# Joining the two words of a float64 weight with one two-input integer operation, the sign moved by a parametric ReLU

## The chip, the cores and the metric

One core of a Trainium2 chip runs the whole program. The metric is device time in microseconds (us), median over runs. Five engines work side by side, each in its own program order: TensorE (PE, with its weight loads as PEld), VectorE (DVE), ScalarE (ACT), GpSimd (POOL) and SyncE (SP, here only a DMA queue).

## The reference, cut to what matters

The inputs are float32 activations and float64 weights. Attention with queries averaged in pairs is followed by two feed-forward blocks on 1152 tokens of 512 numbers:

```
attn = softmax(scale * mean2(q) @ k.T) @ v          # 2 x 8 heads
xn   = x / sqrt(mean(x*x) + 1e-6) * rms_g
x    = (silu(xn @ w_gate) * (xn @ w_val)) @ w_out   # 512 -> 1536 -> 512
h    = x @ w_in
out  = (h * tanh(softplus(h))) @ w_out2             # 512 -> 2048 -> 512
```

## The kernel before, in words

Every product is made of three half-precision matmuls: each factor is split into a high part and the low rest. So each weight block needs a float32 number first, and this kernel makes it from the two 32-bit words of the float64.

**A job** (`w1_job`, `wo_job`, `w2i_job`, `w2o_job`; 68 in all) treats 512 numbers for each of 128 partitions. `w_load` brings both words by DMA into a `raw` tile (four buffers), word 0 the low and word 1 the high one. `w_a` (L395) reads the high word as a float32 and multiplies it by 2^-111 on ACT into `gx` (two buffers); that takes 111 from its exponent field. `w_b` (L401) makes the float32 pattern on DVE into `c` (two buffers) with three operations: L408 shifts `gx` left by 3 and clears the top bit, L411 puts the sign bit of `gx` in, L414 puts the upper three bits of the low word in. `w_c` (L418) rounds `c` to the high part on ACT (L421) and takes the low part by a subtraction on POOL (`lo_op`, L134).

**The order** is written out by hand; every engine takes its instructions in the order of the program. There are four stretches:

- Attention, to about 257 us: 72 steps (`attn_step`). DVE takes row maxima (L267) out of PSUM, ACT the exponentials (L274) and the split of them (L287, L314). Four jobs run here, in pieces (`job_piece`, L449): one call of `w_b` in a step, so the three operations of L408, L411 and L414 fall in three steps, and the fourth step has `w_c` of this job and `w_a` of the next. Each piece stands at the end of its step.
- The first block's two input products, from 258 to 411 us: a unit (`unit1`) is 24 matmuls of 288 columns into two of six PSUM buffers (`pg`, `pv`). ACT applies silu (L572), DVE multiplies (`fo`, L574) and so sets the two buffers free, ACT and POOL split the product (L581, L134). After each unit `job_step` (L434) issues `w_c` of the job two back, `w_b` of the one before, `w_a` of the current one and the load of a later one. So `fo` of a unit stands on DVE behind the operations of the job of the step before.
- The first block's output product, to 484 us: `unit1o` is 36 matmuls of 288 columns into one of the six buffers, set free by `y` on DVE (L136, called from L613). In the first six units two jobs are treated each.
- The second block, from 484 us: 48 steps of 12 matmuls of 384 columns (`h_mm`), mish on ACT (L648), a split on ACT and DVE, and 9 matmuls of 512 columns (`o_part`), with a job in each of the first steps while there are any.

Activation tables are loaded at L758, twice at L572, at L840 and at L894.

Of the kernel before, what the change touches and what calls it, by code (L numbers as in the profile page):

```python
# [9 lines left out]
F32 = mybir.dt.float32  # L10
F16 = mybir.dt.float16
I32 = mybir.dt.int32
ACTF = mybir.ActivationFunctionType
ALU = mybir.AluOpType
# [26 lines left out]
def kernel(  # L41
# [13 lines left out]
    nc = tc.nc  # L55
# [339 lines left out]
    def w_a(job):  # L395
        t = job["raw"]
        gx = raw_p.tile([128, t.shape[1], t.shape[2]], F32, tag="gx", name="gx")
        nc.scalar.activation(out=gx, in_=t[:, :, :, 1].bitcast(F32), func=ACTF.Copy, scale=2.0 ** -111)
        job["g"] = gx

    def w_b(job, part=None):  # L401

        t, g = job["raw"], job["g"].bitcast(I32)
        if part in (None, 0):
            job["c"] = raw_p.tile([128, t.shape[1], t.shape[2]], I32, tag="c", name="c")
        c = job["c"]
        if part in (None, 0):
            nc.vector.tensor_scalar(out=c, in0=g, scalar1=3, scalar2=0x7FFFFFFF,  # L408
                                    op0=ALU.logical_shift_left, op1=ALU.bitwise_and)
        if part in (None, 1):  # L410
            nc.vector.scalar_tensor_tensor(out=c, in0=g, scalar=-0x80000000, in1=c,  # L411
                                           op0=ALU.bitwise_and, op1=ALU.bitwise_or)
        if part in (None, 2):
            nc.vector.scalar_tensor_tensor(out=c, in0=t[:, :, :, 0], scalar=29, in1=c,  # L414
                                           op0=ALU.logical_shift_right, op1=ALU.bitwise_or)
            del job["raw"], job["g"]

    def w_c(job):  # L418
        hi, lo = job["to"]()
        cf = job.pop("c").bitcast(F32)  # L420
        nc.scalar.activation(out=hi, in_=cf, func=ACTF.Copy)  # L421
        lo_op(job.get("eng", nc.gpsimd), lo, cf, 1.0, hi)

    jobs = []
    jn = [0, 0, 0, 0]

    def job_load(upto):
        while jn[0] < min(upto, len(jobs)):
            jobs[jn[0]]["raw"] = jobs[jn[0]]["load"]()
            jn[0] += 1  # L430
# [3 lines left out]
    def job_step(k=1):  # L434

        for _ in range(k):
            if jn[3] < jn[2]:
                w_c(jobs[jn[3]])
                jn[3] += 1
            if jn[2] < jn[1]:  # L440
                w_b(jobs[jn[2]])
                jn[2] += 1
            if jn[1] < len(jobs):
                job_load(jn[1] + 1)
                w_a(jobs[jn[1]])
                jn[1] += 1
            job_load(jn[1] + AHEAD)

    def job_piece(k):  # L449

        i, p = divmod(k, 4)
        if p == 0 and i:
            w_c(jobs[i - 1])
            jn[3] += 1
        if i == NE:
            return
        if p == 0:
            w_a(jobs[i])
            jn[1] += 1
            job_load(jn[1] + AHEAD)  # L460
        elif p == 1:
            w_b(jobs[i], 0)
        else:
            w_b(jobs[i], p - 1)
            jn[2] += p == 3


    ss_t, rw = {}, {}
# [288 lines left out]
    with tc.manual_schedule():  # L757
# [25 lines left out]
        for n in range(NIT):  # L783
            attn_step(n)
            if rs:
                rs.pop(0)()
            if n == RMS0:
                rs = rms_steps(0, 0, NI + 1, 2)
            if n == JOBL:
                job_load(AHEAD)  # L790
            if 0 <= n - JOB0 <= 4 * NE:
                job_piece(n - JOB0)
# [98 lines left out]
        m_p = pool("m", 3)  # L891
        ot_p = pool("ot", 2)

        nc.scalar.preload_act_table_set("mish")  # L894
        hs = [(c, f) for c in range(NC) for f in range(F2)]
        PARTS = 8
        NO = CH // 128
# [50 lines left out]
```

## Time and profile before

| | |
|---|---|
| three runs | 674.79, 675.17, 677.33 us; median 675.17 |
| profiled execution, first to last instruction | 674.8 us |
| mean granted TensorE clock | 0.987 |
| busy: PE, PEld | 605.0 us (90%), 421.6 us (62%) |
| busy: DVE, ACT, POOL | 449.9 (67%), 392.4 (58%), 328.3 us (49%) |
| chain that ended last, by engine | PE 49%, DVE 28%, ACT 8%, issue 8%, DMA 4%, POOL 2% |

The page gives no time around the span, so the span stands for the profiled execution; it is within 0.4 us of the median. A matmul's record is longer than the distance to the next one, since matmuls are pipelined, so how full PE is has to be read from starts and counts. An operation's record includes the time for which it is held up after it was issued.

### The profile page before, as it was taken

Reading aid. Unit: us, or ns where it says so; the run is one execution under the profiler, and the core shown is the slowest. Engines: PE = TensorE matmul, PEld = TensorE weight load, DVE = VectorE, ACT = ScalarE, POOL = GpSimd, SP = SyncE. Lnnn points to the kernel's source line nnn. Section 1 sums busy time; section 2 is a strip of 40 time slices with the busy share of each in tenths; the row PEclk is TensorE's granted clock in tenths of the full one; section 3 lists DMA queues with packets and bytes.
Section 4 is the critical chain, followed back from the end, with each engine's and each line's share of the span. In section 5 each row is a group of like instructions: output and inputs, shape, how many; then the busy total and the mean of one; then the engine's idle time right before and its main releaser. Section 6 shows DMA issues by size and latency. Waiting matters only on the chain.

```text
span 674.8 us, 14672 instructions
## 1 busy us (share of the span) xinstructions
PE 605.0 (90%) x5880; PEld 421.6 (62%) x5880; DVE 449.9 (67%) x740; ACT 392.4 (58%) x659; POOL 328.3 (49%) x260
## 2 busy tenths in 40 slices
PE   3688888888867788899999999999999999999997
PEld 2466566666645567677777677777755555555553
DVE  3889998989969996769999922488299911111110
ACT  4888898998968887655555541344356623223221
POOL 0778878688889752467878741344133300000000
PEclk9899999999988899999999999999999999999999
DMA  6799999999998997625555512156055101001001
GB/s 190 123 211 189 186 183 185 197 182 186 204 203 163 174 161 147 132 94 157 159 157 169 158 47 63 39 182 187 17 169 159 64 0 48 1 1 32 16 1 47
DMA packets 161908, 84.05 MB, mean 125 GB/s; under 512 B 124720, under 2 KB 152368, under 8 KB 161840
## 3 DMA queue, kind: packets, MB, share of 16 engines
q1 hardware_dynamic: 151184, 67.71, 47.0%
q10 hardware_dynamic: 10656, 15.40, 8.4%
q8 instruction: 46, 0.75, 0.5%
q14 instruction: 22, 0.18, 0.1%
HBM read 50.07 MB, written 2.36 MB: 78 GB/s over the span
## 4 chain that ended last, share of the span: by engine, by line
PE 49%; DVE 28%; ACT 8%; issue 8%; DMA 4%; POOL 2%; ACTq 1%; SPq 0%; DVEq 0%; POOLq 0%
DVE m L267 8%; DVE c L411 6%; PE z L544 5%; PE z L546 5%; PE z L545 5%; PE po L681 4%; PE po L680 4%; PE po L679 4%; ACT e L274 3%; PE py L544 3%; PE py L546 3%; PE py L545 3%; DVE c L408 3%; DMA et<-hl 3%; DVE et L134 2%
## 5 line engine op out<-in xcount | busy, mean ns | idle before, releaser
L134 POOL TENSOR_TENSOR hl<-e,hl 128x768 f16<-128x768 f32 x71 | 117.5, 1655 | 60.5 <-ACT hl L287 37.0
L267 DVE TENSOR_REDUCE m<-s 128x1 f32<-128x1152 f32 x72 | 97.3, 1351 | 8.9 <-PE s L249 7.6
L274 ACT ACTIVATE e<-s,m 128x1152 f32<-128x1152 f32 x72 | 87.7, 1218 | 18.8 <-DVE m L268 17.6
L249 PE MATMUL s<-kqT 128*128 128x384 f16 (+1 forms) x480 | 87.9, 336 | 9.6 <-DVE kqT L203 7.5
L136 DVE SCALAR_TENSOR_TENSOR g<-mo,g 128x384 f16<-128x384 f32 x48 | 26.9, 562 | 100.5 <-ACT g L654 100.5
L411 DVE SCALAR_TENSOR_TENSOR c<-gx,c 128x512 int32<-128x512 int32 x68 | 75.7, 1114 | 2.2
L338 PE MATMUL av<-vv,et 128*128 128x65 f16 (+1 forms) x720 | 75.4, 195 | 1.8 <-DMA et<-hl 1.0
L134 POOL TENSOR_TENSOR stretch<-c,stretch 128x512 f16<-128x512 f32 x40 | 51.3, 1283 | 52.0 <-ACT stretch L421 51.8
L414 DVE SCALAR_TENSOR_TENSOR c<-raw,c 128x512 int32<-128x512 int32 x68 | 75.0, 1103 | 2.2
L340 PE MATMUL av<-vv,et 128*128 128x64 f16 (+1 forms) x720 | 75.3, 194 | 0.0
L341 PE MATMUL av<-vv,et 128*128 128x65 f16 (+1 forms) x720 | 75.1, 196 | 0.0
L338 PEld LDWEIGHTS <-et 128*128 128x128 f16 (+1 forms) x720 | 68.0, 102 | 3.6 <-issue 2.3
L340 PEld LDWEIGHTS <-et 128*128 128x128 f16 (+1 forms) x720 | 67.8, 101 | 0.8
L341 PEld LDWEIGHTS <-et 128*128 128x128 f16 (+1 forms) x720 | 67.8, 101 | 0.0
L134 POOL TENSOR_TENSOR h<-fo,h 128x288 f16<-128x288 f32 x48 | 48.8, 1016 | 36.3 <-ACT h L581 36.3
L648 ACT ACTIVATE mo<-z 128x384 f32<-128x384 f32 x48 | 23.3, 484 | 71.3 <-PE z L546 71.3
L287 ACT ACTIVATE hl<-e 128x768 f16<-128x768 f32 x72 | 60.7, 843 | 3.5 <-DMA et<-hl 1.4
L544 PE MATMUL z<-y,w2i 128*128 128x384 f16 x192 | 62.6, 326 | 0.0
L545 PE MATMUL z<-y,w2i 128*128 128x384 f16 x192 | 62.6, 326 | 0.0
L546 PE MATMUL z<-y,w2i 128*128 128x384 f16 x192 | 62.6, 326 | 0.0
L309 PE MATMUL ep<-idf,e 128*128 128x128 f32 x216 | 39.0, 291 | 24.7 <-ACT e L274 23.5
L249 PEld LDWEIGHTS <-kqT 128*128 128x128 f16 (+1 forms) x480 | 40.2, 102 | 33.1 <-issue 15.6
(106 smaller groups left out, 1570.0 us busy)
## 6 DMA issues: line engine op xcount, KB each, us to landing
raw<-in_moe_w_out_dram SPq DMA_DIRECT2D x28, 512.0 KB, 3.4
raw<-in_moe_w_in_dram SPq DMA_DIRECT2D x16, 512.0 KB, 3.7
raw<-in_moe_w_gate_dram SPq DMA_DIRECT2D x8, 512.0 KB, 3.6
raw<-in_moe_w_val_dram SPq DMA_DIRECT2D x8, 512.0 KB, 3.5
vn<-in_v_dram ACTq DMA_DIRECT2D x14, 288.0 KB, 2.9
kn<-in_k_dram ACTq DMA_DIRECT2D x12, 288.0 KB, 4.5
qn<-in_q_dram ACTq DMA_DIRECT2D x12, 256.0 KB, 3.4
raw<-in_moe_w_gate_dram ACTq DMA_DIRECT2D x4, 512.0 KB, 5.0
```

What stands on the lines that cost most here:

```text
L134: eng.tensor_tensor(out=out_, in0=in_, in1=hi, op=ALU.subtract)
L249: mm = nc.tensor.matmul(out=ps[p0:p0 + m, c, 0:SN], lhsT=qt[:, w * NTI + slot, p0:p0 + m], rhs=kt[:, e * NJ + c * per:e * NJ + (c + 1) * p ...
L267: nc.vector.tensor_reduce(out=m[:, 0:1], in_=ps[:, :, 0:SN], op=ALU.max, axis=AXL.XY, negate=True)
L274: nc.scalar.activation(out=e.rearrange("p (c s) -> p c s", c=SC), in_=ps[:, :, 0:SN], func=ACTF.Exp, bias=m[:, 1:2], scale=s_scale)
L338: nc.tensor.matmul(out=av[0:m, o0:o0 + D + 1], lhsT=hi, rhs=vr[:, D:2 * D + 1], start=(jj == 0), stop=False)
L340: nc.tensor.matmul(out=av[0:m, o0:o0 + D], lhsT=hi, rhs=vr[:, 0:D], start=False, stop=False)
L341: nc.tensor.matmul(out=av[0:m, o0:o0 + D + 1], lhsT=et[:, z + (NB if jj < NB else PB), p0:p0 + m], rhs=vr[:, D:2 * D + 1], start=False, st ...
L411: nc.vector.scalar_tensor_tensor(out=c, in0=g, scalar=-0x80000000, in1=c, op0=ALU.bitwise_and, op1=ALU.bitwise_or)
L414: nc.vector.scalar_tensor_tensor(out=c, in0=t[:, :, :, 0], scalar=29, in1=c, op0=ALU.logical_shift_right, op1=ALU.bitwise_or)
L544: nc.tensor.matmul(out=ps, lhsT=w0, rhs=x0, start=(i == 0), stop=False)
L545: nc.tensor.matmul(out=ps, lhsT=w0, rhs=x1, start=False, stop=False)
L546: nc.tensor.matmul(out=ps, lhsT=w1, rhs=x0, start=False, stop=(i == n - 1))
```

## The change

`w_a` uses a parametric ReLU with the factor -(2^32) on negative numbers in place of a copy. A negative number comes out positive with 32 added to its exponent field, so that bit 28 of `gx` carries the sign, and a shift left by 3 brings it to bit 31. `w_b` has two operations: the low word is shifted right by 29 into `c`, and `gx` shifted left by 3 is joined with it. The low word's shift reads every second word of `raw`. In the pieces of the attention stage the two operations take the places of the first and the second, and the third place is empty. The activation table loaded ahead of the second block is named `mish_and_others`, not `mish`.

```
-        nc.scalar.activation(out=gx, in_=t[:, :, :, 1].bitcast(F32), func=ACTF.Copy, scale=2.0 ** -111)
+        nc.scalar.activation(out=gx, in_=t[:, :, :, 1].bitcast(F32), func=ACTF.Prelu, scale=2.0 ** -111,
+                             alpha=-(2.0 ** 32))
...
         if part in (None, 0):
-            nc.vector.tensor_scalar(out=c, in0=g, scalar1=3, scalar2=0x7FFFFFFF,
-                                    op0=ALU.logical_shift_left, op1=ALU.bitwise_and)
+            nc.vector.tensor_scalar(out=c, in0=t[:, :, :, 0], scalar1=29, scalar2=None,
+                                    op0=ALU.logical_shift_right)
         if part in (None, 1):
-            nc.vector.scalar_tensor_tensor(out=c, in0=g, scalar=-0x80000000, in1=c,
-                                           op0=ALU.bitwise_and, op1=ALU.bitwise_or)
-        if part in (None, 2):
-            nc.vector.scalar_tensor_tensor(out=c, in0=t[:, :, :, 0], scalar=29, in1=c,
-                                           op0=ALU.logical_shift_right, op1=ALU.bitwise_or)
+            nc.vector.scalar_tensor_tensor(out=c, in0=g, scalar=3, in1=c,
+                                           op0=ALU.logical_shift_left, op1=ALU.bitwise_or)
             del job["raw"], job["g"]
...
-        elif p == 1:
-            w_b(jobs[i], 0)
-        else:
+        elif p < 3:
             w_b(jobs[i], p - 1)
-            jn[2] += p == 3
+            jn[2] += p == 2
...
-        nc.scalar.preload_act_table_set("mish")
+        nc.scalar.preload_act_table_set("mish_and_others")
```

## Rows read from the trace of the kernel before

**Rows 1.** Busy time by stretch: us, then PE, PEld, DVE, ACT, POOL busy, PEclk, DMA.
```profile
320.00:340.00 20.00, 20.00 (x165) 15.96 (x164) 19.59 (x26) 11.17 (x25) 15.29 (x12) 1.00 0.51 159
360.00:380.00 20.00, 18.66 (x148) 14.13 (x146) 19.55 (x26) 11.22 (x26) 15.39 (x13) 1.00 0.52 159
520.00:540.00 20.00, 20.00 (x110) 10.55 (x108) 18.60 (x24) 11.97 (x25) 7.77 (x7) 1.00 0.26 80
```

**Rows 2.** Waits of PE, 255 to 675 us: total us, times, longest.
```profile
PE pv L544 <- DVE fo L574: 2.3, 5, 0.5
PE py L544 <- DVE y L136: 1.9, 2, 1.0
PE pv L546 <- POOL stretch L134: 1.2, 1, 1.2
```

**Rows 3.** Timeline of PE around two of its waits: start, us, instruction, [idle before].
```profile
283.96 0.29 PE L545 MATMUL pv<-stretch 128*128 128x288 f16 x1
285.48 0.30 PE L546 MATMUL pv<-stretch 128*128 128x288 f16 x1 [1.24 <-POOL stretch L134]
...
358.98 0.29 PE L546 MATMUL pg<-stretch 128*128 128x288 f16 x1
359.73 0.28 PE L544 MATMUL pv<-stretch 128*128 128x288 f16 x1 [0.46 <-DVE fo L574]
```

**Rows 4.** Groups by line and shape, whole span: busy us, mean ns, idle before.
```profile
L411 DVE SCALAR_TENSOR_TENSOR c<-gx,c 128x512 int32<-128x512 int32 x68 | 75.7, 1114 | 2.2
L414 DVE SCALAR_TENSOR_TENSOR c<-raw,c 128x512 int32<-128x512 int32 x68 | 75.0, 1103 | 2.2
...
L398 ACT ACTIVATE gx<-raw 128x512 f32<-128x512 f32 x68 | 45.1, 666 | 0.0
...
L408 DVE TENSOR_SCALAR c<-gx 128x512 int32<-128x512 int32 x68 | 37.7, 554 | 19.5 <-POOL woh L134 15.6 <-ACT gx L398 2.9 <-POOL w2i L134 1.0
...
L141 DVE TENSOR_SCALAR vn<-vn 128x1152 f32<-128x1152 f32 x7 | 5.3, 753 | 0.0
...
L516 ACT ACTIVATE xh<-xn,w 128x512 f16<-128x512 f32 x4 | 2.8, 714 | 2.4 <-DVE xn L507 2.4
...
L572 ACT ACT_TABLE_LOAD x2 | 2.6, 1283 | 0.0
...
L516 ACT ACTIVATE xh<-xn 128x512 f16<-128x512 f32 x4 | 2.5, 631 | 0.1
```

**Rows 5.** Timeline of DVE, two units of the first block.
```profile
302.76 0.44 DVE L574 SCALAR_TENSOR_TENSOR fo<-ft,pv 128x288 f32<-128x288 f32 x1
...
303.74 1.54 DVE L411 SCALAR_TENSOR_TENSOR c<-gx,c 128x512 int32<-128x512 int32 x1
305.32 1.10 DVE L414 SCALAR_TENSOR_TENSOR c<-raw,c 128x512 int32<-128x512 int32 x1
306.34 0.44 DVE L574 SCALAR_TENSOR_TENSOR fo<-ft,pv 128x288 f32<-128x288 f32 x1
...
307.15 0.69 DVE L411 SCALAR_TENSOR_TENSOR c<-gx,c 128x512 int32<-128x512 int32 x1
...
309.34 0.44 DVE L574 SCALAR_TENSOR_TENSOR fo<-ft,pv 128x288 f32<-128x288 f32 x1
```

**Rows 6.** Timeline of POOL, beside those units, and one product's low part alone.
```profile
289.54 0.73 POOL L134 TENSOR_TENSOR h<-fo,h 128x288 f16<-128x288 f32 x1 [0.59 <-ACT h L581]
...
303.58 1.16 POOL L134 TENSOR_TENSOR stretch<-c,stretch 128x512 f16<-128x512 f32 x1
```

**Rows 7.** Timeline of ACT in attention: exponentials behind the steps with L414.
```profile
227.73 1.22 ACT L274 ACTIVATE e<-s,m 128x1152 f32<-128x1152 f32 x1 [0.20 <-DVE m L268]
...
240.35 1.22 ACT L274 ACTIVATE e<-s,m 128x1152 f32<-128x1152 f32 x1 [0.37 <-DVE m L268]
...
252.96 1.22 ACT L274 ACTIVATE e<-s,m 128x1152 f32<-128x1152 f32 x1 [0.34 <-DVE m L268]
```

**Rows 8.** Timeline of DVE at the first block's start.
```profile
281.88 1.10 DVE L414 SCALAR_TENSOR_TENSOR c<-raw,c 128x512 int32<-128x512 int32 x1
```

## The prediction

> **What bounds the kernel now.** I read the busy time by stretch first, then the waits of PE, then the timelines of the engines that it waits for. The reader is to see that the kernel has three regimes, and that only two of them can give anything back.
>
> From 484 us on, PE is never idle although DVE is 93% busy (the third row) [rows 1]. Nothing that DVE does less of there is worth anything. In the first block's input products PE is at its limit too at first: 165 matmuls in 20 us are 0.121 us each, so a unit of 24 takes 2.91 us at full granted clock [rows 1]. But DVE needs longer: two units start 6.58 us apart, 3.29 us each, without a gap [rows 5]. PE runs ahead of DVE by its six PSUM buffers until they are used up; then it issues fewer matmuls in a stretch (the second row) [rows 1] and waits for `fo` five times. So DVE is the bound there, with PE close behind. The list of waits names all that PE loses to DVE's work on weights: `fo` five times, `y` twice, and once a low part of a weight that POOL makes late because DVE was late [rows 2]. In attention PE waits for ACT and DVE in turn; there the reader looks at ACT's exponentials and at what was still missing when they started [rows 7].
>
> **What it removes.** One of three DVE operations of a job goes, 68 in all. By its record each of the two-input ones is 1.10 to 1.11 us on average [rows 4], so DVE loses some 75 us of busy time. Very little of that is on the path. Stage by stage:
>
> *Attention, four jobs.* The step with L414 loses it. The next exponential on ACT had waited for DVE for 0.20, 0.37 and 0.34 us in three of these steps [rows 7]; in the fourth ACT had no such wait. Behind these waits ACT is the next late one (exponential, split and transposed part follow each other without a gap), so what goes is the wait and not the whole operation: 0.9 us. Bounds: 0 if the PE or a transposing DMA is late instead, and 4 x 1.10 = 4.4 us if DVE is the only bound. I take 0.9, since the rows show the wait itself.
>
> *Start of the first block.* PE stands from one matmul to the next for 1.52 us where 0.12 is normal, a loss of 1.40 us, for the low part of a weight [rows 3]. Ahead of that part stand L414 with 1.10 us [rows 8], ACT's rounding, and POOL's subtraction, which is at 1.16 us when it meets no DVE operation [rows 6] and meets one here. With L414 gone the chain is 1.10 us shorter, and somewhat more where POOL collides less. I take 1.3; bounds 1.0 and 1.4, since PE can't get back more than it lost.
>
> *Units with a job.* Each of the five waits for `fo` is a gap of 0.75 us between starts in place of 0.12 [rows 3], so 5 x 0.63 = 3.1 us. A unit on DVE now holds `fo` 0.44, L408 0.55 [rows 4], and L411 and L414, of which one meets POOL in turn: 1.54 + 1.10 in one unit, 0.69 and a longer one in the next [rows 5]. Without one of them a unit is 0.44 + 0.55 + 1.54 = 2.5 us at the most. PE needs 2.91 and becomes the bound; all 3.1 us go. What is late next is PE itself; ACT has 11.2 us of work in 20 and POOL 15.3 [rows 1], which at 2.91 us a unit instead of 3.29 become 63% and 87%.
>
> *Output product.* The two waits for `y` are 1.9 us by the list and about 0.17 us more each, since a matmul's record reaches 0.17 us (0.29 - 0.12) past the next start: 2.2 us. A unit with two jobs costs DVE 2 x (0.55 + 1.11 + 1.10) + 0.44 = 6.0 us by the means [rows 4], PE 36 x 0.121 = 4.4. Without one operation DVE is at 3.8, so it no longer leads; I take the whole 2.2, and 1 as a lower bound, since all collisions may fall on the operation that is left.
>
> *Second block:* nothing, PE covers it [rows 1]. If that cover were gone, the removal could only help.
>
> **What it adds or alters.** The shift of the low word takes L408's place. It reads words at a distance of 8 bytes, which L408 doesn't. The nearest row is L141, which scales 1152 numbers in place at that distance in 0.753 us [rows 4], 0.65 ns each; at that rate 512 take 0.33 us and the start, so it costs what L408 does. Bounds: 0.2 us less than L408's mean of 0.55, which has held-up ones in it, and, at the price of an unblocked two-input operation, 0.69 [rows 5], 0.14 more; a unit is still below 2.91. Its wait changes from `gx` to `raw`, which lands before `gx` is made; the wait for POOL to leave the `c` buffer stays as it is, with the joining operation and the next `fo` queued behind it as before. The joining operation now waits for `gx`, which ACT writes a step earlier. `raw` comes free one operation earlier, so a load may go out a microsecond sooner; DMA is half busy here [rows 1] and this is worth nothing. SP's queue has only those loads in it then.
>
> The parametric ReLU on ACT: no row shows it. The copy in its place takes 0.67 us. The nearest row for a dearer form of the same size is L516 with a factor per partition, 0.714 against 0.631 us without [rows 4], 0.08 more; a doubling, 0.67 more, is the far end. I take 0 to 0.08: on the path it counts only in attention, 4 times, so 0.3 us at most (2.7 for the doubling), and in the units ACT has room.
>
> The port that DVE and POOL share is worth a look. A two-input operation on DVE lasts 0.69 us alone and 1.54 us beside a subtraction on POOL that had started earlier [rows 5, 6]: the first one in holds the other up. The Trainium skill, page "SBUF — State Buffer", section "Who interferes with whom", says that such operations lock a shared pair of ports for a whole instruction. By that rule alone a unit before would have been 0.73 + 1.16 + 0.55 + 0.69 + 0.69 = 3.82 us where 3.29 is measured, so the trace agrees with the lock but not with its full length. By the rule a unit after would be 3.13 us, above PE's 2.91, and a part of the five waits could stay, which is the first rival below; by the rows it is under 2.91 and none stays.
>
> **Sum.** 0.9 + 1.3 + 3.1 + 2.2 = 7.5 us, less 0.1 for the ReLU: 7.4. The profiled execution has 674.8 us and goes to 667.4; the median of the runs is 0.4 us above it, so I say 667.8. With the bounds of the terms (0 to 4.4, 1.0 to 1.4, 3.1, 1.0 to 2.2, less 0.3 or nothing) the gain is 4.8 to 11.1, and the time 664.1 to 670.4.
>
> **The rivals.**
>
> *The collision stays.* POOL's operations now meet the one two-input operation and the shift each time, and the unit stays near 3.25 us. Of the first block's 30 jobs 27 follow each other in this way (the others fall into its start). Before, DVE's lag was 27 x (3.29 - 2.91) = 10.3 us and cost PE 3.1, so the buffers and the start hid 7.2. At 3.25 us the lag is 27 x 0.34 = 9.2, 2.0 above what is hidden, so only 1.1 of the 3.1 goes, and of the 2.2 perhaps 1. Gain 0.9 + 1.0 + 1.1 + 1.0 = 4.0 or, with a term of attention lost, 2: 671 to 673. For it: POOL would be 87% busy. Against it: with 0.69 us less to hold, it needs an operation that gets longer than any that is shown in the units.
>
> *Hidden anyway.* The gain in attention is swallowed by a DMA, and PE finds another wait (silu, the product's low part on POOL) at each place. Gain 0 to 2: about 674. For it: much of DVE's busy time was off the path. Against: the waits of PE for DVE and for what hangs on it have a sum of 6.7 us and name the operation in front.
>
> *Slower: the ReLU is not in the table that silu or mish use.* Then ACT loads a table before each ReLU and another before the next silu, 2 x 1.28 us [rows 4]. A unit has 11.17 / 6.1 = 1.84 us of ACT work [rows 1], with the loads 4.40 us against 3.29: it decides as soon as ACT passes 2.91, and it would. Some 30 units: +33 us; 14 steps of the second block at 11.97 / 5.2 + 2.57 = 4.87 against 3.84: +14; four times 2.57 in attention: +10. About 730. For it: the edit names another table ahead of mish, so the tables differ in what they hold. Against: copies and squares run beside silu, exponentials and mish, and the trace has five loads in all, so simple functions sit in several tables. The Trainium skill, page "ScalarE: Activation LUTs", section "What ACT_TABLE_LOAD costs", gives 2.66 us for a switch with its drain, which would make a unit 7.2 us and the whole some 100 us dearer still; the rows show 1.28 us and no idle time ahead of it.
>
> **How the numbers follow.** Forecast 0.72, the collision stays 0.13, hidden anyway 0.10, slower by tables 0.05. One measurement tells 0.5% from no change, 3.4 us. Faster by more: the forecast and half of the first rival, 0.78. Within: the other half and nearly all of the second, 0.16. Slower: the tables and a remainder, 0.06. The range 664.0 to 672.7 holds the forecast and most of the first rival.
>
> **What would show it right or wrong.** PE's waits for `fo` at L574 and for `y` are gone from the list, and the one for POOL's low part is under 0.3 us. A unit takes 2.91 us on PE with DVE idle in it; DVE's busy time falls from 450 to about 375 us. The ReLU's row reads about 0.67 us, and the table loads are five. The prediction is wrong if loads multiply, if the two operations of a job last over 2.4 us together in the units, or if attention ends later than before.

## The result and the profile after

The change makes the kernel slower: median 681.0 us (679.8 to 681.8) against 675.95 (674.8 to 677.3), ratio 1.0067 with a 95% interval of 1.0046 to 1.0089. Forecast was 667.8. The profiled execution has a span of 678.8 us against 674.8; its run took 680.6, so 1.8 us lie around the span, more than the 0.4 that I had assumed for the kernel before.

The table cuts the spans at the first matmul of each stage (start of `pg`, `py` and `z` in the timeline of PE). In it the whole story can be seen: up to the second block 7.8 us are gained, near the forecast, and the second block gives 11.8 back.

| kernel | attention ends | input products | output product | second block | span |
|---|---|---|---|---|---|
| before | 258.0 | 153.2 | 72.7 | 190.9 | 674.8 |
| after | 257.1 | 147.9 | 71.1 | 202.7 | 678.8 |

First the busy times of the kernel after by stretch (columns as in [rows 1]):

```profile
320.00:340.00 20.00, 20.00 (x165) 15.98 (x164) 17.45 (x21) 13.52 (x28) 14.90 (x14) 1.00 0.62 188
...
360.00:380.00 20.00, 20.00 (x166) 15.96 (x164) 14.30 (x18) 11.24 (x24) 13.56 (x14) 1.00 0.51 159
...
520.00:540.00 20.00, 17.30 (x92) 8.73 (x91) 10.77 (x13) 19.76 (x26) 6.14 (x5) 1.00 0.32 106
```

In the second row PE has its 166 matmuls where it had 148 [rows 1]. In the third it has 92 where it had 110, and ACT went from 12.0 to 19.8 us of 20: a new bound, and not the engine that the change was aimed at. The groups by line and shape, whole span, say with what ACT is busy:

```profile
L414 DVE SCALAR_TENSOR_TENSOR c<-gx,c 128x512 int32<-128x512 int32 x68 | 80.2, 1179 | 3.7 <-ACT gx L400 1.1
...
L411 DVE TENSOR_SCALAR c<-raw 128x512 int32<-128x512 int32 x68 | 52.2, 767 | 26.6 <-POOL woh L134 24.4 <-POOL w2i L134 2.1
...
L400 ACT ACTIVATE gx<-raw 128x512 f32<-128x512 f32 x68 | 45.3, 669 | 0.2
...
L646 ACT ACT_TABLE_LOAD x16 | 20.5, 1283 | 0.3
L570 ACT ACT_TABLE_LOAD x2 | 2.6, 1283 | 0.0
...
L400 ACT ACT_TABLE_LOAD x15 | 19.2, 1283 | 0.3
```

(The change shifts lines: L400 is the ReLU, L411 the shift of the low word, L414 the joining; L570 is silu and L646 mish.) The ReLU costs what the copy did, 669 against 666 ns [rows 4]. But 31 table loads of 1.283 us have come: one ahead of nearly each ReLU in the second block and one ahead of the mish behind it. Beside silu there are two, as before. The timeline of ACT shows one step of the second block:

```profile
484.81 0.49 ACT L646 ACTIVATE mo<-z 128x384 f32<-128x384 f32 x1
485.20 0.52 ACT L652 ACTIVATE g<-mo 128x384 f16<-128x384 f32 x1
485.61 0.62 ACT L421 ACTIVATE stretch<-c 128x512 f16<-128x512 f32 x1
486.25 1.28 ACT L400 ACT_TABLE_LOAD   x1
487.55 0.68 ACT L400 ACTIVATE gx<-raw 128x512 f32<-128x512 f32 x1
488.25 1.28 ACT L646 ACT_TABLE_LOAD   x1
489.54 0.49 ACT L646 ACTIVATE mo<-z 128x384 f32<-128x384 f32 x1
```

From mish to mish are 4.73 us without a gap. PE needs 3.84 for the step by the prediction's figure, and 3.89 by its starts: these two of `z` in the kernel before are two steps apart, 7.79 us.

```profile
513.16 0.33 PE L544 MATMUL z<-y,w2i 128*128 128x384 f16 x1
...
520.95 0.33 PE L544 MATMUL z<-y,w2i 128*128 128x384 f16 x1
```

PE's waits in the kernel after, from 255 us on (as in [rows 2]):

```profile
PE z L542 <- ACT mo L646: 9.4, 8, 1.3
PE pg L542 <- DMA stretch<-xh: 1.6, 1, 1.6
PE ep L309 <- ACT e L274: 1.2, 1, 1.2
...
PE py L542 <- DVE y L136: 0.2, 1, 0.2
```

The three waits of [rows 2] are gone, but for 0.2 us, and one for mish has come.

### The profile page after: what moved, and what is told of

Its sections match the earlier page's. It is cut to its first block, busy times and chain, and to the rows that moved or that the text cites. A ratio compares the mean times of both kernels' runs of the same rounds, so it can differ in the third digit from the quotient of the medians.

```text
span 678.8 us, 14635 instructions
## 1 busy us (share of the span) xinstructions
PE 605.0 (89%) x5880; PEld 420.5 (62%) x5880; DVE 399.0 (59%) x672; ACT 437.1 (64%) x690; POOL 318.1 (47%) x260
## 4 chain that ended last, share of the span: by engine, by line
PE 55%; ACT 20%; DVE 15%; issue 4%; DMA 3%; POOL 2%; ACTq 1%; SPq 0%; DVEq 0%; POOLq 0%
DVE m L267 7%; ACT e L274 5%; PE z L542 3%; PE z L544 3%; PE z L543 3%; PE pg L542 3%; PE pg L543 3%; PE pv L544 3%; PE pv L543 3%; PE pv L542 3%; PE pg L544 3%; PE po L677 3%; PE po L679 3%; PE po L678 3%; PE py L542 3%
## 5 line engine op out<-in xcount | busy, mean ns | idle before, releaser
L414 DVE SCALAR_TENSOR_TENSOR c<-gx,c 128x512 int32<-128x512 int32 x68 | 80.2, 1179 | 3.7 <-ACT gx L400 1.1
L134 POOL TENSOR_TENSOR stretch<-c,stretch 128x512 f16<-128x512 f32 x40 | 49.9, 1247 | 68.7 <-ACT stretch L421 68.4
L338 PE MATMUL av<-vv,et 128*128 128x65 f16 (+1 forms) x720 | 74.7, 194 | 2.3 <-DMA et<-hl 1.4
L341 PE MATMUL av<-vv,et 128*128 128x65 f16 (+1 forms) x720 | 74.3, 195 | 0.0
L411 DVE TENSOR_SCALAR c<-raw 128x512 int32<-128x512 int32 x68 | 52.2, 767 | 26.6 <-POOL woh L134 24.4
L134 POOL TENSOR_TENSOR h<-fo,h 128x288 f16<-128x288 f32 x48 | 45.4, 946 | 43.7 <-ACT h L579 43.7
L646 ACT ACTIVATE mo<-z 128x384 f32<-128x384 f32 x48 | 23.5, 490 | 63.5 <-PE z L544 63.2
```

The lines of the kernel that those rows point to most:

```text
L134: eng.tensor_tensor(out=out_, in0=in_, in1=hi, op=ALU.subtract)
L338: nc.tensor.matmul(out=av[0:m, o0:o0 + D + 1], lhsT=hi, rhs=vr[:, D:2 * D + 1], start=(jj == 0), stop=False)
L341: nc.tensor.matmul(out=av[0:m, o0:o0 + D + 1], lhsT=et[:, z + (NB if jj < NB else PB), p0:p0 + m], rhs=vr[:, D:2 * D + 1], start=False, st ...
L414: nc.vector.scalar_tensor_tensor(out=c, in0=g, scalar=3, in1=c, op0=ALU.logical_shift_left, op1=ALU.bitwise_or)
```

## The experiments

Theory: the switch of tables between ReLU and mish is the whole loss, and the operation taken from DVE is a gain everywhere ahead of it. Rivals: the ReLU or the order on DVE costs in the second block; the earlier start of the block costs; the new table's name is at fault.

**Only the second block in the old way.** `w_a` and `w_b` of the 16 `w2o` jobs as before, and the old name of the table:

```
+        if job.get("old"):
+            nc.scalar.activation(out=gx, in_=t[:, :, :, 1].bitcast(F32), func=ACTF.Copy, scale=2.0 ** -111)
...
+            "to": lambda: (w2o[:, z:z + 1, 0, :], w2o[:, z:z + 1, 1, :]), "old": True}
...
-        nc.scalar.preload_act_table_set("mish_and_others")
+        nc.scalar.preload_act_table_set("mish")
```

> The 16 jobs of the second block (w2o) are made in the old way, copy and three operations, with the table named mish; all other jobs as in the changed kernel. Theory (table loads between the ReLU and mish are the whole loss, the two-operation form is a gain everywhere else): no loads beyond five; h_mm starts at about 476.3 us as in the changed kernel and takes the 191.0 us that it took before, so a span near 667.3 and a time near 668, ratio to before 0.989. Rival (the new form also costs something in the second block or after it, such as weights that come late): span above 670.

Measured: 668.65 us, ratio 0.9891 (0.9871 to 0.9910), span 666.4; five loads; second block 190.8 us. Both parts of the theory hold, and the number forecast for the change is met by the change without its second block.

**Only the second block in the new way**, the complement (the flag inverted, three pieces in attention):

> The complement: the new form for the second block's 16 jobs alone, all others in the old form. Theory: h_mm starts at 483.8 as before, then 31 table loads and 11.5 us more: span near 686.3, ratio 1.017. Rival (the loss needs PE's earlier start, or is in the first block): span within 3 us of 674.8.

Measured: 688.8 us, ratio 1.0182 (1.0159 to 1.0206), span 688.3. Its second block takes 202.8 us after a start at 485.5, so the earlier start has no part in the loss. The span is 2.0 us above the expected one, of which 1.6 are in attention, ahead of its first job, where the code is that of the kernel before. Its PE waits show the old ones and the new one together:

```profile
PE z L555 <- ACT mo L659: 9.5, 8, 1.3
PE pv L555 <- DVE fo L585: 2.3, 5, 0.5
PE py L555 <- DVE y L136: 1.9, 2, 1.0
...
PE pv L557 <- POOL stretch L134: 1.2, 1, 1.2
```

**Silu in the place of mish**, the ReLU in all jobs:

```
-        nc.scalar.activation(out=o, in_=ps[:, 0:CH], func=ACTF.Mish, scale=1.0 / (Y_S * W_S))
+        nc.scalar.activation(out=o, in_=ps[:, 0:CH], func=ACTF.Silu, scale=1.0 / (Y_S * W_S))
-        nc.scalar.preload_act_table_set("mish_and_others")
+        nc.scalar.preload_act_table_set("silu_and_others")
```

> The changed kernel with silu in the place of mish in the second block (so the output is not the reference's) and the table named silu_and_others ahead of it; everything else the same, the ReLU in all 68 jobs. Theory (only the switch of tables costs, not the ReLU and not the two operations): no load at L646 or L400, second block near 191 us, span near 667. Rival (the ReLU itself or DVE's order costs in the second block): span stays near 678.

Measured: 669.4 us, ratio 0.9884 (0.9859 to 0.9910), span 667.6, second block 190.9, no load at either line. The ReLU and the two operations cost nothing in the second block; the rival falls.

**The old name of the table** in the changed kernel:

> The changed kernel with the table ahead of the second block named mish again. Theory: the name decides only the first load; one more load before the first ReLU behind it, loads at every job as before, time within 1.3 us of the changed kernel's (ratio 1.007 to 1.010). Rival (the new name caused the loads): loads are gone and the span is near 667.

Measured: 682.4 us, ratio 1.0089 (1.0069 to 1.0109). The group of loads at the ReLU has 16 in place of 15, and the second block takes 204.2 us, 1.5 more. So `mish` is the table that serves mish and not the ReLU, and the one named in the change serves the ReLU and not mish; neither of the two names spares the switches. No run tried a third.

**The third operation again**, on top of the first experiment (e1 below):

```
+        if part in (None, 2):
+            nc.vector.scalar_tensor_tensor(out=c, in0=t[:, :, :, 0], scalar=29, in1=c,
+                                           op0=ALU.logical_shift_right, op1=ALU.bitwise_or)
```

> As e1 (the second block's 16 jobs in the old way), but the other 52 jobs get a third operation on DVE again, the old last one, which writes bits that stand there already; the ReLU stays. Theory (the gain up to the second block is the operation taken from DVE and nothing else): PE's waits for fo (5), for y (2) and for POOL's low part are back, h_mm starts near 483.8 us, span near 674.8, ratio to before 0.997 to 1.003. Rival (a part of the gain comes from the ReLU in the place of a copy, or from raw and gx coming free in another order): span 668 to 672.

Measured: ratio 1.000 (0.9986 to 1.0014), span 674.8, second block's start at 483.9. PE's waits are those of [rows 2]:

```profile
PE pv L558 <- DVE fo L588: 2.3, 5, 0.5
PE py L558 <- DVE y L136: 2.0, 2, 1.1
...
PE pv L560 <- POOL stretch L134: 1.4, 1, 1.4
```

The ReLU by itself is neutral; the gain is the operation on DVE.

**Half of the loads**, in two ways: two ReLUs side by side in every second step (four `gx` buffers), or every second job in the old way (e7 below):

```
+            if hn % 2 == 0:
+                for _ in range(2):
...
+                        w_a(jobs[jn[1]])
```

> The changed kernel, but in the second block two ReLUs are issued side by side in every second step (four gx buffers), one rounding and one joining in each step. Theory (a load costs only as far as it lifts ACT's work in a step above PE's 3.84 us): some 16 loads in place of 31 beyond the five; two steps hold 2 x 2.2 + 2.6 = 7.0 us on ACT against 7.7 on PE, so nearly all of the 11.5 us comes back, span 667 to 669. Rival (each load costs its share, 11.5 / 31 = 0.37 us): 16 loads cost 5.9, span near 673.

> The changed kernel, but every second of the second block's 16 jobs is made in the old way (copy, three operations): some 15 loads in place of 31. Theory: as for the pairs, ACT's mean over two steps is below PE's, and PE is at most one step ahead short by a load: span 667 to 669. Rival (each load costs its share): span near 673.

Measured: 669.5 us, ratio 0.9884 (0.9859 to 0.9910), span 665.9; and 668.1, 0.9881 (0.9849 to 0.9912), span 665.7. Both have 15 loads (8 + 7) in the second block, and both need 190.9 us for it: half of the loads cost not half of the loss but nothing. The timeline of ACT in the kernel with pairs shows why:

```profile
490.28 1.28 ACT L400 ACT_TABLE_LOAD   x1
491.57 1.24 ACT L400 ACTIVATE gx<-raw 128x512 f32<-128x512 f32 x2
492.83 1.28 ACT L646 ACT_TABLE_LOAD   x1
494.12 0.49 ACT L646 ACTIVATE mo<-z 128x384 f32<-128x384 f32 x1
...
495.44 0.48 ACT L646 ACTIVATE mo<-z 128x384 f32<-128x384 f32 x1
...
497.55 0.63 ACT L421 ACTIVATE stretch<-c 128x512 f16<-128x512 f32 x1 [1.22 <-DVE c L414]
```

Two steps hold two loads, and ACT still waits 1.22 us for DVE in them. It has room again, so PE is the bound.

**Attention.** The gain there was a term of the sum that one comparison of spans can't settle: in the trace that each run left, six kernels without the third operation enter the first block between 255.8 and 258.4 us (mean 257.0), three with it at 257.5 to 259.6. So the step got it back once, and three times:

> As e7, but the four jobs of attention have the old last operation again in the step where it stood, writing bits that stand there already. The starts of the first block seen so far are 257.5 to 259.6 us in three kernels with that operation and 255.8 to 258.4 in six without it. Theory (each costs what ACT then waits, 0.9 in all): first block starts 0.9 later than in e7, about 256.8. Rival (attention covers it): as e7, 255.8. One look can tell neither from the spread; it is the reference of the next one.

> As e8 with that operation three times in the step, 12 more two-input operations in attention than e7. Theory (behind the first 0.5 us that ACT covers, DVE is the bound of such a step): 4 x (3 x 0.75 - 0.5) = 7 us, first block starts near 263. Rival (attention is bound by PE, ACT or DMA there and hides DVE's work): start below 258.5.

Measured, in one execution each: start at 258.8 and at 268.0 us; the rest of these spans (409.9) agrees with that of every second job in the old way to 0.1 us. The starts of the kernel with twelve operations and of every second job in the old way (255.8) are 12.2 us apart, where 7 were expected: attention hides less of DVE than I thought. The timelines of DVE and of ACT in the last kernel show one such step:

```profile
229.48 3.52 DVE L433 SCALAR_TENSOR_TENSOR c<-raw,c 128x512 int32<-128x512 int32 x3
232.92 1.34 DVE L267 TENSOR_REDUCE m<-s 128x1 f32<-128x1152 f32 x1
...
234.55 1.22 ACT L274 ACTIVATE e<-s,m 128x1152 f32<-128x1152 f32 x1 [2.26 <-DVE m L268]
```

Three operations hold the row maximum up by 3.5 us, where three unblocked ones would be 3 x 0.69 = 2.1, and the exponential waits 2.26. For a single operation in a step all four kernels with it start the first block at 257.5 to 259.6 us (mean 258.5), 1.5 later than the mean of the six without, and the two spreads overlap.

The spread, however, lies ahead of the first job's operations on DVE, where nothing of the edits has come but one ReLU: the first of them starts between 198.2 and 200.8 us. So I measure from that operation to the first matmul of the first block, in the kernel before and then in the one after:

```profile
199.15 1.63 DVE L408 TENSOR_SCALAR c<-gx 128x512 int32<-128x512 int32 x1
257.98 0.29 PE L544 MATMUL pg<-stretch 128*128 128x288 f16 x1
...
199.51 1.63 DVE L411 TENSOR_SCALAR c<-raw 128x512 int32<-128x512 int32 x1
257.10 0.29 PE L542 MATMUL pg<-stretch 128*128 128x288 f16 x1
```

| kernels | from the first job to the first block |
|---|---|
| four with the operation once in the step | 58.79 to 58.83 us |
| six without it | 57.56 to 57.60 us |
| one with it three times | 69.05 us |

Seen this way there is no overlap: the operation, once in each of four jobs, costs 1.2 us in attention, and three times in each it costs 11.5.

## Why the prediction was wrong

**The step that failed** is the line on the second block: "nothing, PE covers it. If that cover were gone, the removal could only help." The first half is true of DVE, for which it was worked out. The change also puts another function on ACT in that stage, and the edit was priced by the length of one ReLU (0 to 0.08 us more than the copy; measured 0.003), not by what ACT has to load between it and its neighbours. PE's cover over ACT there was 3.84 - 2.30 = 1.54 us a step; two loads are 2.57.

**The case itself was among the rivals, with the wrong chance and too wide a place.** It had 0.05. For mish its mechanism was right and its size nearly: 4.87 us a step forecast and 4.73 measured, +14 forecast and 11.8 measured. PE stands in 14 steps, as many as were forecast, but loses 4.73 - 3.89 = 0.84 us in each on average and not 1.03; its first wait for mish comes at 490.1 us, 14 us into the block. For silu it was wrong: no load there, and none between exponentials. What was held against it, that copies and squares run beside all three functions without a load, says nothing of a ReLU with a factor; that was an inference from two functions to a third. What spoke for it, that the edit renames the table of just one stage, got little weight, and the prediction didn't ask whether the table so named serves mish. It doesn't, and by the experiment with the old name that one doesn't serve the ReLU. (The dearer sum at the end of that rival is wrong by its own price: 48 units and steps at 7.2 - 4.4 = 2.8 us more are some 130 us and not 100. Nothing of it was seen.)

**The terms of the sum** came near the forecast, 7.5 us up to the second block against 7.8. Attention: 0.9 forecast and 0.9 between these two traces, but that they agree is luck, since the first job starts 0.36 us later in the one after; from the first job on it is 1.2. The gain is where the waits were: 0.32 us up to the third job's first operation on DVE, 0.47 from there to the fourth's and 0.45 behind it, each 0.1 us more than the wait of [rows 7] there (0.20, 0.37, 0.34). Start of the first block and units: 4.4 forecast, 5.3 measured (153.2 to 147.9). The wait for POOL's low part went altogether, 1.4 in place of the 1.3 taken; the rest, some 0.8, lies in gaps of 0.15 to 0.40 us from start to start between 353 and 390 us, which carry no releaser in the trace of before and are gone after. (POOL's subtraction of 1.16 us, read there as one that meets no DVE operation, has L411 beside it [rows 5, 6]; it is one that DVE doesn't hold up.) Output product: 2.2 forecast, 1.6 measured (72.7 to 71.1); one wait of 0.17 us and one gap stay.

**The first rival was half right.** The collision with POOL did stay, and moved to another operation. L408 alone in the kernel before, two units on DVE in the changed kernel, and POOL's subtractions of weights beside them:

```profile
300.12 0.42 DVE L408 TENSOR_SCALAR c<-gx 128x512 int32<-128x512 int32 x1
...
320.01 0.46 DVE L572 SCALAR_TENSOR_TENSOR fo<-ft,pv 128x288 f32<-128x288 f32 x1
320.38 0.42 DVE L411 TENSOR_SCALAR c<-raw 128x512 int32<-128x512 int32 x1
320.84 1.53 DVE L414 SCALAR_TENSOR_TENSOR c<-gx,c 128x512 int32<-128x512 int32 x1
322.95 0.45 DVE L572 SCALAR_TENSOR_TENSOR fo<-ft,pv 128x288 f32<-128x288 f32 x1 [0.58 <-PE pv L544]
323.32 1.23 DVE L411 TENSOR_SCALAR c<-raw 128x512 int32<-128x512 int32 x1
324.59 1.10 DVE L414 SCALAR_TENSOR_TENSOR c<-gx,c 128x512 int32<-128x512 int32 x1
325.89 0.46 DVE L572 SCALAR_TENSOR_TENSOR fo<-ft,pv 128x288 f32<-128x288 f32 x1 [0.20 <-PE pv L544]
...
320.61 1.21 POOL L134 TENSOR_TENSOR woh<-c,woh 128x512 f16<-128x512 f32 x1 [1.29 <-ACT woh L421]
...
323.11 1.16 POOL L134 TENSOR_TENSOR w2i<-c,w2i 128x512 f16<-128x512 f32 x1
```

The shift is 0.42 us alone, as L408 was, and 1.23 us where a subtraction on POOL started before it. So it takes over a collision that L411 had met in such a unit (1.54 us [rows 5]), and it is outside the bounds that the prediction gave it (0.35 to 0.69). A unit holds DVE for up to 0.46 + 1.23 + 1.10 = 2.79 us, where 2.5 was to be the most. These longer operations are for the most part why DVE's busy time fell from 449.9 to 399.0 us and not to 375: the shift has a mean of 767 ns, L408 had 554, and the joining has 1179, L411 had 1114, together some 19 us in 68 jobs. But two units take 5.88 us, 2.94 each, with 0.58 and 0.20 us idle in which DVE waits for PE: PE is the bound, as the forecast said, and 3.25 us for a unit, which that rival needed, was not reached. The second rival, that the gain stays hidden, fell with the gains of the table.

## What to carry to other kernels

A function that takes another's place on ACT is priced by the table beside which it runs, stage by stage, not by its own length: count the loads that the order of calls makes, and compare ACT's work in a step, loads included, with the engine that bounds the step. Loads within that room are free (15 cost nothing, 31 cost 11.8 us), so pair the calls, or keep the old form in the one stage where the tables differ. When an edit changes a name in one stage only, ask what that stage has which the others lack, and don't take the rename for the answer.

## What the runs showed of the hardware

A load is 1.283 us in every group of the traces, whichever table it loads, and the function behind it starts 0.01 to 0.02 us after its end. The Trainium skill, page "ScalarE: Activation LUTs", section "What ACT_TABLE_LOAD costs", gives 2.66 us with a drain. The trace doesn't agree: by an estimate from that price a step with two loads would be 7.5 us, and it takes 4.73.

The ReLU with a factor costs 669 ns for 128x512, as a copy does. A shift that reads every second word and writes densely costs 0.42 us for 128x512, as the dense one did, and 1.15 to 1.29 us in the units where a subtraction on POOL had started before it.
